# Row turning by transposes, logits and table products in column tiles, one-hots on ScalarE

## Chip, cores and metric

The kernel runs on one core of a Trainium2 chip. The metric is the device time of one execution in microseconds (us), as a median of several runs; less is better.

## What is computed

Two blocks follow each other. The first is a state-space scan (Mamba-2 form) over x (4 batches, 8 heads, 768 tokens, 32 values a head), with a decay per token, and with B and C of 16 state values. The second is a router with eight experts over the 4 x 768 = 3072 rows that come out, each of 8 x 32 = 256 values:

```python
# block 1, per batch and head, over 24 chunks of 32 tokens
L = exp(cum_i - cum_j) * causal
y = (C B^T * L) x  +  (C state) * exp(cum)
state = decay_full * state + sum_j decay_from_j * B_j x_j
# block 2, per row of y
xn = x / (norm(x) + 1e-6);  en = emb / (norm(emb) + 1e-6)
logits = xn @ en.T / tau
e = argmax(logits);  gate = softmax(logits)[e]
out = gate * (relu(x @ w1[e]) @ w2[e])
```

All data are 32-bit floats; w1 is 256 x 1024 and w2 1024 x 256 for each expert.

## The kernel before

**Chunks.** The scan works in six chunks of 128 tokens, each with all four batches at once (`mamba`, L705, loop at L745). One pass of the loop is called a step. In step c TensorE multiplies inside the chunk (`inner`), VectorE masks the products (`mask_inner`, L372), TensorE adds the part from the states (`from_states`) and the outputs (`outputs`, `first_outputs`), and ScalarE copies the result out of PSUM as `yT` (`keep_outputs`, L424), with the 256 values of a row along the partitions. GpSimd scales x and the states (L276, L289, L324); VectorE adds the states up (`add_sums`, L347).

**Rows.** `finish` (L427) turns chunk c − 1 back, so that tokens lie along the partitions. For each batch b and each half z of the 256 values it multiplies `yT` by `turn`, which holds an identity with permuted columns and, beside it, eight columns of the normalised expert embedding: rows and logits come out of one product of 136 columns, in the banks `py[0]`, `py[1]`, `pz[0]`, `pz[1]`. `keep_rows` (L441, L443) copies them to SBUF on ScalarE and `send_rows` writes them to DRAM (`y_rows`). In steps 3 and 4 `finish` is called in two parts, with `locate` between them; in the other steps, and in `scan_end`, in one go.

**Places.** `pick` finds each row's expert (VectorE), `count_picks` counts (GpSimd), `rank_rows` and `keep_ranks` give each row its rank in its expert (TensorE, ScalarE), and `places` (L581, VectorE) turns the rank into a place: a tile of 104 rows (one of four, `NT`) and a place in it (`p`). It makes two one-hots: `eq`, 32 columns (expert, tile) with the row's number, and `hot`, 104 columns with a one at the row's place (L614). `locate` (L620) multiplies them, summed over the four batches of a chunk, to a table of 104 x 32: for each place of each expert the number of the row that goes there. Chunk c − 2 is placed in step c and located one step later. Tables of the first chunks are kept and added (`keep_located` on ScalarE, `add_located` on GpSimd). In the last step `early_places` (L913) makes a first table from three chunks, and GpSimd gathers the first rows of two experts with it. `end_places` (L643) completes the table.

**The scan's end** (`scan_end`, L853) mixes the last chunks' rows and places with the first expert's products, in this order of calls: `up(0)`; ranks of chunk 4; `up(1)`; `finish`, `keep_rows` and `send_rows` of chunk 5; places of chunk 4; pick of chunk 5; `up(2)`, square, `up(3)`, square; `locate` of chunks 3 and 4; `up(4)`; ranks and places of chunk 5; `up(5)`, square, `up(6)`, square; the gates' power, largest and scale; `up(7)`; the second expert's `turn_x`; the gates' exp; `down(0)`; `locate` of chunk 5; `end_places`; the late gathers; `down(1)`. An `up` is four TensorE instructions into one of four PSUM banks, which a Relu on ScalarE (L1049) empties; `down` sums eight such results.

**Experts.** Then `moe` (L1315) takes one expert after the other. Each weight w1 comes as two transfers of 512 KB on the SP queue (`load_weights`, L82), w2 as one of 1 MB; three buffers of each are in use.

**What sets the order.** The scan, `scan_end` and `moe` are under a manual schedule: on every engine, instructions stand in the order in which the code calls them, and an engine takes them in that order. The framework adds the waits for data and for buffers.

Of the kernel before, what the change touches and what calls it, by code (L numbers as in the profile page):

```python
# [16 lines left out]
NB, NH, S, D, N = 4, 8, 768, 32, 16  # L17
# [5 lines left out]
DM, E, F = NH * D, 8, 1024  # L23
KD, KF = DM // 128, F // 128
TR, NT = 104, 4
# [6 lines left out]
LG, Y1, W = 128, 128 + E, DM + E  # L32
# [46 lines left out]
    )  # L79


def load_weights(k, e, parts=(0, 1), after=None):  # L82
    nc = k.nc
    i = slice(e, e + 1)
    if e >= FIXED:
        i = bass.ds(
            nc.values_load(
                k.order[0:1, e - FIXED : e - FIXED + 1], engines=(mybir.EngineType.SP,), min_val=0, max_val=E - 1
            ), 1,
        )  # L90
    if 0 in parts:
        k.w1t[e] = k.wp.tile([128, KD, F], F32, name="w1", tag="w1")
        for v in range(2):
            d = nc.sync.dma_start(
                k.w1t[e][64 * v : 64 * v + 64],
                k.w1[i, 128 * v : 128 * v + 128, :].rearrange("o (z p) f -> p (o z) f", z=KD),
            )
            if after is not None:
                hold(k, d, after)
    if 1 in parts:  # L100
        k.w2t[e] = k.wp.tile([128, KF, DM], F32, name="w2", tag="w2")
        d = nc.sync.dma_start(k.w2t[e][:], k.w2[i].rearrange("o (f p) m -> p (o f) m", p=128))
        if after is not None and 0 not in parts:
            hold(k, d, after)
# [319 lines left out]
        t.kept = k.nc.scalar.copy(out=t.yT[:, z].rearrange("p b s -> p (b s)"), in_=k.py[:, z, :])  # L424


def finish(k, c, parts=(0, 1)):  # L427
    yT = k.ld[c].yT
    banks = (((2, k.py[:, 0]), (3, k.py[:, 1])), ((0, k.pz[0]), (1, k.pz[1])))
    for b, ps in [x for p in parts for x in banks[p]]:  # L430
        for z, at in ((0, 0), (1, LG)):
            k.nc.tensor.matmul(
                ps[:, at : at + Y1], lhsT=yT[:, z, b, :], rhs=k.turn[:, z, :],
                start=(z == 0), stop=(z == 1), skip_group_check=True,
            )


# [23 lines left out]
def square_emb(k):  # L461
    nc = k.nc
    sq = k.mc.tile([E, DM], F32, name="emb_sq")
    r = k.en_r = k.mc.tile([E, 1], F32, name="emb_r")
    nc.scalar.activation(sq[:], k.en[:], ACT.Square, accum_out=r[:])
    nc.gpsimd.tensor_tensor(out=r[:], in0=r[:], in1=k.half[0:E, 0:1], op=ALU.pow)
    k.turn = k.mc.tile([128, KD, Y1], F32, name="turn")
    for z, at in ((0, 0), (1, E)):
        nc.gpsimd.tensor_copy(
            out=k.turn[:, z, at : at + 128].rearrange("p (v r d) -> p v r d", v=2, r=2),  # L470
            in_=k.ident[:].rearrange("p (r v d) -> p v r d", r=2, v=2),
        )


def scale_emb(k):
# [14 lines left out]
def turn_emb(k, ps):  # L490


    nc = k.nc
    for z in range(KD):
        nc.tensor.transpose(ps[:, E * z : E * z + E], k.en2[:, z, :], k.ident[:E, :E])
    for z, at in ((0, 128), (1, 0)):
        nc.scalar.copy(out=k.turn[:, z, at : at + E], in_=ps[:, E * z : E * z + E])


def route_consts(k):  # L500
    nc = k.nc

    def ints(name, shape, pattern, base, by, dtype=F32):
        i = k.mc.tile(shape, I32, name=name + "_i")
        nc.gpsimd.iota(i[:], pattern=pattern, base=base, channel_multiplier=by)
        f = k.const.tile(shape, dtype, name=name)
        nc.gpsimd.tensor_copy(out=f[:], in_=i[:])
        return f

# [12 lines left out]
    k.ones = k.const.tile([128, 128], BF16, name="ones_b")  # L522
    nc.gpsimd.tensor_copy(out=k.ones[:], in_=ones)
    k.before = k.const.tile([128, 128], BF16, name="before_b")
    nc.gpsimd.tensor_copy(out=k.before[:], in_=before)
    k.ob = k.const.tile([128, NU, E], BF16, name="ob")
    k.pre = k.const.tile([128, NU + 1, E], BF16, name="pre")
    nc.gpsimd.memset(k.pre[:, 0, :], 0.0)
    k.s1 = k.const.tile([128, NU], F32, name="s1")
    k.idx = k.const.tile([TR, E * NT], F32, name="idx")  # L530
    k.shifted = k.mc.tile([128, E], F32, name="shifted")
    nc.gpsimd.memset(k.shifted[:], 0.0)
    nc.gpsimd.memset(k.shifted[0:1, 0:2], 1.0)
    k.at, k.eq, k.hot = {}, {}, {}
# [46 lines left out]
def places(k, c):  # L581


    nc = k.nc
    w = k.work
    be = [128, NB, E]
    u = slice(NB * c, NB * c + NB)
    v = k.at.pop(c)
    nc.vector.scalar_tensor_tensor(
        out=v[:], in0=v[:], scalar=1.0, in1=k.ob[:, u, :], op0=ALU.add, op1=ALU.mult  # L590
# [9 lines left out]
    nc.vector.scalar_tensor_tensor(  # L600
        out=p[:], in0=p[:], scalar=-float(TR), in1=k.s1[:, u], op0=ALU.mult, op1=ALU.add
    )
    nc.vector.tensor_tensor(out=v[:], in0=v[:], in1=p[:].unsqueeze(2).to_broadcast(be), op=ALU.subtract)
    eq = k.eq[c] = w.tile([128, NB * E, NT], F32, name="eq", tag="eq")
    nc.vector.tensor_tensor(
        out=eq[:], in0=v[:].rearrange("p b e -> p (b e)").unsqueeze(2).to_broadcast([128, NB * E, NT]),
# [7 lines left out]
    nc.vector.tensor_tensor(  # L614
        out=hot[:], in0=k.place_at[:].unsqueeze(1).to_broadcast([128, NB, TR]),
        in1=p[:].unsqueeze(2).to_broadcast([128, NB, TR]), op=ALU.is_equal,
    )


def locate(k, c, first=True, last=True):  # L620

    eq, hot = k.eq.pop(c), k.hot.pop(c)
    for b in range(NB):
        k.nc.tensor.matmul(  # L624
            k.pz[0][:TR, 424 : 424 + E * NT], lhsT=hot[:, b, :],
            rhs=eq[:].rearrange("p (b e) t -> p b (e t)", b=NB)[:, b], start=(first and b == 0),
            stop=(last and b == NB - 1), skip_group_check=True,
        )


def keep_located(k, c):
    i = k.idx
    if c > 0:
        i = k.ix = k.work.tile([TR, E * NT], F32, name="ix", tag="ix")
    k.nc.scalar.copy(out=i[:], in_=k.pz[0][:TR, 424 : 424 + E * NT])


def add_located(k, c):
    if c > 0:
        k.nc.gpsimd.tensor_tensor(out=k.idx[:], in0=k.idx[:], in1=k.ix[:], op=ALU.add)  # L640


def end_places(k):  # L643
    nc = k.nc
    n = k.pz[1][:, 456 : 456 + E]
    nc.tensor.matmul(n, lhsT=k.ones[:], rhs=k.pre[:, NU, :], start=True, stop=True)
    nc.vector.tensor_tensor(out=k.idx[:], in0=k.idx[:], in1=k.pz[0][:TR, 424 : 424 + E * NT], op=ALU.add)
    k.gi = k.const.tile([TR, E * NT], I32, name="gi")
    k.to = k.const.tile([TR, E * NT], I32, name="to")
    to_rows(k, k.idx[:, 0 : FIXED * NT], 0)  # L650
    k.n = k.const.tile([128, E], F32, name="n")
    nc.vector.tensor_copy(out=k.n[:], in_=n)
# [260 lines left out]
def early_places(k, c):  # L913

    nc = k.nc
    ps = k.pz[0][:TR, 424 : 424 + E * NT]
    locate(k, c)
    nc.vector.tensor_tensor(out=k.idx[:], in0=k.idx[:], in1=ps, op=ALU.add)
    gi = k.ep.tile([TR, E * NT], I32, name="gi0")
    nc.vector.tensor_scalar(out=gi[:], in0=k.idx[:], scalar1=-1.0, scalar2=0.0, op0=ALU.add, op1=ALU.max)  # L920
    k.gi0 = gi


# [562 lines left out]
def leftover(k):  # L1486


    nc = k.nc
# [4 lines left out]
    with k.tc.If(blocks > 0):  # L1494
# [22 lines left out]
        with k.tc.For_i(0, blocks, 1) as i:  # L1517
            e = nc.values_load(table[0:1, 0, bass.ds(i, 1)], engines=(SP,), min_val=0, max_val=E - 1)
            w1 = k.wp.tile([128, KD, F], F32, name="w1", tag="w1")
            for v in range(2):  # L1520
                nc.sync.dma_start(
                    w1[64 * v : 64 * v + 64], k.w1[bass.ds(e, 1), 128 * v : 128 * v + 128, :].rearrange(
                        "o (z p) f -> p (o z) f", z=KD
                    )
                )
# [136 lines left out]
```

## Time and profile before

| | |
|---|---|
| median of three runs | 259.28 us (258.48 to 259.39) |
| the profiled execution | 257.48 us |
| its span, first to last instruction | 255.6 us |
| TensorE (PE) busy | 240.7 us |
| VectorE (DVE) busy | 174.7 us |
| ScalarE (ACT) busy | 109.8 us |
| GpSimd (POOL) busy | 128.4 us |
| turning products, L432 | 96 instructions, 14.0 us |
| table products, L624 | 48 instructions, 5.1 us |

The profile shows one execution. PE counts matmuls, PEld the loading of their weights, which overlaps them. A line such as "L624 PE MATMUL pz<-eq,hot 128*104 128x32 f32 x48 | 5.1, 253" names the line of the code, the engine, what is written from what, the shape, how often, the busy time in us and the mean duration of one in ns; instructions overlap, so the mean is more than the spacing. A 32-bit product appears as two instructions. "idle before" with an arrow tells how long the engine stood still and what released it. The chain of waits is followed back from the last instruction: start, length, what; "issue" is time for which nothing that the profile shows was awaited. In the row of digits each digit is a fortieth of the span, in tenths of busy time.

### The profile page before, as it was taken

How to read it: one execution, taken by the hardware profiler on the slowest of the kernel's cores; microseconds unless marked ns; L12 is line 12 of the kernel's file. 1: busy time of each engine (PE TensorE's matmuls, PEld its weight loads, DVE VectorE, ACT ScalarE, POOL GpSimd, SP SyncE). 2: the span in 40 equal slices, each digit the busy share in tenths (PEclk: the TensorE clock that was granted, in tenths of full speed). 3: DMA queues.
4: the chain of work that ended last, by engine and by line, in shares of the span. 5: the costliest groups of instructions: out<-in, count | busy, mean ns of one | idle time of the engine just before them, and what ended most of it. 6: DMA issues, size and time to landing. Idle time of an engine off the chain costs nothing.

```text
span 255.6 us, 6715 instructions
## 1 busy us (share of the span) xinstructions
PE 240.7 (94%) x2589; PEld 222.5 (87%) x2590; DVE 174.7 (68%) x467; ACT 109.8 (43%) x308; POOL 128.4 (50%) x173
## 2 busy tenths in 40 slices
PE   7889889998999999999999999999999999999990
PEld 2577778878899999999989999999998999999890
DVE  6776898899655533152978897897987888884121
ACT  2435335353254232341385175367338527538300
POOL 8899564764712552838171168248417526026032
PEclk9999999999999999999999999999999999999999
DMA  4978847327299469698911682393194202001001
GB/s 119 306 227 264 279 111 213 131 84 170 65 293 266 151 140 270 147 258 202 255 49 36 135 244 72 88 253 107 39 250 142 69 0 54 11 0 52 13 18 40
DMA packets 22322, 35.90 MB, mean 140 GB/s; under 512 B 2553, under 2 KB 15556, under 8 KB 22288
## 3 DMA queue, kind: packets, MB, share of 16 engines
q1 hardware_dynamic: 19024, 28.73, 41.1%
q0 software_dynamic: 3088, 6.67, 9.8%
q8 instruction: 21, 0.34, 0.6%
q14 instruction: 13, 0.11, 0.1%
q10 hardware_dynamic: 176, 0.06, 0.1%
HBM read 29.05 MB, written 6.50 MB: 139 GB/s over the span
## 4 chain that ended last, share of the span: by engine, by line
PE 46%; POOL 19%; issue 17%; DVE 11%; DMA 5%; ACT 1%; POOLq 1%; DVEq 0%; ACTq 0%
PE yp L1204 15%; PE yp L1132 8%; PE hp L1132 5%; PE eb L1045 5%; DMA out_dram<-yo,to 5%; PE eb L1063 4%; POOL xb L289 4%; POOL xg L934 3%; DVE g L372 3%; POOL out_dram L1255 2%; POOL xs L276 2%; POOL spread L121 1%; PE yp L1032 1%; PE pz L624 1%; PE hp L1045 1%
## 5 line engine op out<-in xcount | busy, mean ns | idle before, releaser
L1255 POOL DMA_INDIRECT out_dram<-yo,to x32 | 34.0, 1063 | 65.1 <-ACT yo L1252 37.2
L934 POOL DMA_INDIRECT xg<-y_rows,gi x32 | 37.3, 1166 | 17.1 <-issue 8.8
L372 DVE TENSOR_TENSOR g<-pg,mask 128x1536 f32<-128x1536 f32 x12 | 21.1, 1754 | 5.5 <-PE pg L362 5.5
L1150 ACT ACTIVATE hT<-hT 128x416 f32<-128x416 f32 (+5 forms) x36 | 19.0, 532 | 12.4 <-DVE hT L1154 11.4
L1063 PE MATMUL yp<-hT,w 128*128 128x208 f32 (+1 forms) x128 | 22.1, 329 | 0.5 <-ACT hT L1150 0.5
L1063 PEld LDWEIGHTS yp<-hT,w 128*128 128x128 f32 x128 | 21.1, 190 | 0.8 <-ACT hT L1150 0.8
L1204 PE MATMUL yp<-T,S 128*128 128x208 f32 (+4 forms) x120 | 21.8, 331 | 0.0
L1282 POOL TENSOR_TENSOR gr<-gr,half 104x4 f32<-104x4 f32 x8 | 9.8, 1219 | 22.0 <-ACT sq L1276 21.9
L1154 DVE TENSOR_TENSOR hT<-hp,u 128x416 f32<-128x416 f32 (+5 forms) x24 | 13.3, 564 | 10.6 <-PE hp L1132 6.5
L1204 PEld LDWEIGHTS yp<-T,S 128*128 128x128 f32 x120 | 20.4, 190 | 0.0
L1132 PE MATMUL yp<-T,S 128*128 128x208 f32 (+5 forms) x96 | 18.6, 336 | 0.4 <-DVE S L1089 0.2
L1132 PEld LDWEIGHTS yp<-T,S 128*128 128x128 f32 x96 | 15.4, 190 | 1.6 <-ACT u L1145 1.1
L1204 PE MATMUL yp<-hT,w 128*128 128x208 f32 (+4 forms) x80 | 15.1, 331 | 0.0
L1145 ACT COPY p<-yp 128x416 f32<-128x416 f32 (+5 forms) x12 | 5.7, 479 | 21.4 <-PE yp L1132 21.4
L1204 PEld LDWEIGHTS yp<-hT,w 128*128 128x128 f32 x80 | 13.7, 190 | 0.0
L1276 ACT ACTIVATE sq<-xg 104x256 f32<-104x256 f32 x32 | 13.0, 408 | 0.0
L1045 PE MATMUL eb<-xT,w 128*128 128x208 f32 x64 | 12.8, 345 | 0.0
L424 ACT COPY yT<-py 128x512 f32<-128x512 f32 x12 | 6.4, 589 | 14.6 <-PE py L413 14.6
L1045 PE MATMUL hp<-xT,w 128*128 128x208 f32 x64 | 12.2, 339 | 0.0
L1063 PE MATMUL eb<-hT,w 128*128 128x208 f32 x64 | 12.0, 341 | 0.0
L1145 ACT COPY u<-yp 128x416 f32<-128x416 f32 (+5 forms) x24 | 11.5, 485 | 1.3 <-PE yp L1132 1.1
L1101 DVE TENSOR_TENSOR T<-hT 128x832 f32<-128x832 f32 (+4 forms) x10 | 9.8, 984 | 3.0 <-ACT hT L1150 3.0
(264 smaller groups left out, 581.3 us busy)
## 6 DMA issues: line engine op xcount, KB each, us to landing
w<-in_moe_w_dram SPq DMA_DIRECT2D x16, 512.0 KB, 6.3
w<-in_moe_w_dram SPq DMA_DIRECT2D x8, 1024.0 KB, 8.2
y_rows<-rows SPq DMA_DIRECT2D x6, 528.0 KB, 5.0
x<-in_x_dram SPq DMA_DIRECT2D x6, 512.0 KB, 6.4
ct<-in_CT_dram SPq DMA_DIRECT2D x6, 256.0 KB, 5.7
bi<-in_BT_dram SPq DMA_DIRECT2D x6, 256.0 KB, 2.8
b<-in_B_dram SPq DMA_DIRECT2D x6, 256.0 KB, 5.2
xa<-in_x_dram SPq DMA_DIRECT2D x6, 128.0 KB, 5.0
```

Source lines behind the costliest of these rows:

```text
L289: engine.tensor_tensor(out=k.xb[c % 2][p, :, :, v, :], in0=src.rearrange("p b (q d) -> p b q d", q=4), in1=r[p, :, 4 * v : 4 * v + 4].unsq ...
L372: t.masked = k.nc.vector.tensor_tensor(out=g[:], in0=k.pg[:, :, 0:384].rearrange("p q (u m) -> p q u m", u=2), in1=k.mask[:].unsqueeze(1). ...
L934: k.nc.gpsimd.indirect_dma_start(out=x, out_offset=None, in_=k.y_d[0:rows, :], in_offset=bass.IndirectOffsetOnAxis(ap=at, axis=0), bounds_ ...
L1045: nc.tensor.matmul(t, lhsT=s.w1[:, j, 128 * f : 128 * f + 128], rhs=s.xT[:, j, 0:m], start=(j == 0), stop=(j == KD - 1))
L1063: nc.tensor.matmul(t, lhsT=s.w2[:, f, 128 * j : 128 * j + 128], rhs=s.hT[:, f, r], start=(f == 0), stop=(f == KF - 1))
L1132: nc.tensor.matmul(t[:, m * u : m * u + m], lhsT=w[:, f : f + 128], rhs=x, start=start and u == 0, stop=True, skip_group_check=True,)
L1145: nc.scalar.copy(out=p[:, 0 : 2 * m], in_=t[:, 0 : 2 * m])
L1150: nc.scalar.activation(h, h, ACT.Relu)
L1154: nc.vector.tensor_tensor(out=h, in0=view(t), in1=view(p), op=ALU.add)
L1204: nc.tensor.matmul(t, lhsT=a[:, f], rhs=b[:, f], start=start and f == 0, stop=(f == 3), skip_group_check=True)
L1255: d = nc.gpsimd.indirect_dma_start(out=k.out[:, :], out_offset=bass.IndirectOffsetOnAxis(ap=s.to[:p, i : i + 1], axis=0), in_=y[:p], in_of ...
L1276: s.k.nc.scalar.activation(sq[:], s.x[:, i, :].rearrange("p (j w) -> p j w", j=KD)[:, :, 0:128], ACT.Square, accum_out=s.r[:, i : i + 1],)
```

## The change

Seven things are edited.

- `finish` turns rows by transposes (one per batch and half) with the plain identity. The values of a row therefore stay in yT's order instead of being permuted.
- The logits are products of their own: the embedding (`emb_t`, padded to 32 columns) times `yT`, one column tile of the array per batch, into `py[0]`. ScalarE copies them to SBUF (`lt`), and four small products turn them into the rows' columns 128 to 135. The transposes of batches 2 and 3 and the logits form part 0, the rest part 1.
- `turn` is gone; `emb_t` is cleared on GpSimd, and one copy on ScalarE instead of two fills it.
- w1 is loaded with its rows permuted to match, by four transfers of 256 KB instead of two of 512 KB.
- `places` makes `hot` on ScalarE: four Squares of (place − p), one per batch, and one Relu of 1 − 2·square. The sign of `p` is turned for that.
- `locate` swaps the operands: `eq` is the stationary one, and each batch has a column tile of its own, so that the sum over batches is not made there. The kept tables are 128 x 104 instead of 104 x 32.
- `table` adds the kept tables to the last one (VectorE) and sums over batches and turns with one product against `same`, four 32 x 32 identities made on GpSimd. `early_places` and `end_places` call it.

```diff
+def w1_rows(k, t, i):
+    issued = []
+    for v in range(2):
+        rows = k.w1[i, 128 * v : 128 * v + 128, :].rearrange("o (z r d) f -> r d (o z) f", z=KD, r=2)
+        for r in range(2):
+            p = 64 * r + 32 * v
+            issued.append(k.nc.sync.dma_start(t[p : p + 32], rows[r]))
+    return issued
...
+def turn_rows(k, c, b, ps):
+    for z, at in ((0, 0), (1, Y1)):
+        k.nc.tensor.transpose(ps[:, at : at + 128], k.ld[c].yT[:, z, b, :], k.ident[:])
...
 def finish(k, c, parts=(0, 1)):
-    yT = k.ld[c].yT
-    banks = (((2, k.py[:, 0]), (3, k.py[:, 1])), ((0, k.pz[0]), (1, k.pz[1])))
-    for b, ps in [x for p in parts for x in banks[p]]:
-        for z, at in ((0, 0), (1, LG)):
+    t = k.ld[c]
+    banks = [k.pz[0], k.pz[1], k.py[:, 0], k.py[:, 1]]
+    if 0 in parts:
+        for b in (2, 3):
+            turn_rows(k, c, b, banks[b])
+        l = k.py[:, 0, W : W + 128]
+        for z in range(KD):
+            for b in range(NB):
+                k.nc.tensor.matmul(
+                    l[32 * b : 32 * b + 32], lhsT=k.emb_t[:, z, :], rhs=t.yT[:, z, b, :], start=(z == 0),
+                    stop=(z == 1), tile_position=(0, 32 * b), skip_group_check=True,
+                )
+        t.lt = k.work.tile([128, 128], F32, name="lt", tag="lt")
+        k.nc.scalar.copy(out=t.lt[:], in_=l)
+    if 1 in parts:
+        for b in (0, 1):
+            turn_rows(k, c, b, banks[b])
+        for b in (2, 3, 0, 1):
+            p = slice(32 * b, 32 * b + 32)
             k.nc.tensor.matmul(
-                ps[:, at : at + Y1], lhsT=yT[:, z, b, :], rhs=k.turn[:, z, :],
-                start=(z == 0), stop=(z == 1), skip_group_check=True,
+                banks[b][:, LG : LG + E], lhsT=t.lt[p], rhs=k.ident[p, 32 * b : 32 * b + E], start=True, stop=True,
+                tile_position=(32 * b, 0), skip_group_check=True,
             )
...
     hot = k.hot[c] = w.tile([128, NB, TR], F32, name="hot", tag="hot")
-    nc.vector.tensor_tensor(
-        out=hot[:], in0=k.place_at[:].unsqueeze(1).to_broadcast([128, NB, TR]),
-        in1=p[:].unsqueeze(2).to_broadcast([128, NB, TR]), op=ALU.is_equal,
-    )
+    for b in range(NB):
+        nc.scalar.activation(hot[:, b, :], k.place_at[:], ACT.Square, bias=p[:, b : b + 1])
+    nc.scalar.activation(hot[:], hot[:], ACT.Relu, bias=1.0, scale=-2.0)
...
     for b in range(NB):
         k.nc.tensor.matmul(
-            k.pz[0][:TR, 424 : 424 + E * NT], lhsT=hot[:, b, :],
-            rhs=eq[:].rearrange("p (b e) t -> p b (e t)", b=NB)[:, b], start=(first and b == 0),
-            stop=(last and b == NB - 1), skip_group_check=True,
+            k.pz[0][32 * b : 32 * b + 32, 400 : 400 + TR],
+            lhsT=eq[:].rearrange("p (b e) t -> p b (e t)", b=NB)[:, b], rhs=hot[:, b, :], start=first, stop=last,
+            tile_position=(0, 32 * b), skip_group_check=True,
         )
...
+def table(k):
+
+    k.nc.vector.tensor_tensor(out=k.idx_t[:], in0=k.idx_t[:], in1=k.pz[0][:, 400 : 400 + TR], op=ALU.add)
+    t = k.pz[1][:TR, 464 : 464 + E * NT]
+    k.nc.tensor.matmul(t, lhsT=k.idx_t[:], rhs=k.same[:], start=True, stop=True, skip_group_check=True)
+    return t
...
-    nc.vector.tensor_tensor(out=k.idx[:], in0=k.idx[:], in1=k.pz[0][:TR, 424 : 424 + E * NT], op=ALU.add)
+    nc.vector.tensor_copy(out=k.idx[:], in_=table(k))
...
     locate(k, c)
-    nc.vector.tensor_tensor(out=k.idx[:], in0=k.idx[:], in1=ps, op=ALU.add)
     gi = k.ep.tile([TR, E * NT], I32, name="gi0")
-    nc.vector.tensor_scalar(out=gi[:], in0=k.idx[:], scalar1=-1.0, scalar2=0.0, op0=ALU.add, op1=ALU.max)
+    nc.vector.tensor_scalar(out=gi[:], in0=table(k), scalar1=-1.0, scalar2=0.0, op0=ALU.add, op1=ALU.max)
```

More of the change, by code (lines that the diff above doesn't have):

```diff
@@ L92, in load_weights @@
         k.w1t[e] = k.wp.tile([128, KD, F], F32, name="w1", tag="w1")
[L93 to L96, printed above, removed]
-            )
+        for d in w1_rows(k, k.w1t[e], i):
             if after is not None:
@@ L466, in square_emb @@
     nc.gpsimd.tensor_tensor(out=r[:], in0=r[:], in1=k.half[0:E, 0:1], op=ALU.pow)
[L467 to L472, printed above, removed]
+    k.emb_t = k.mc.tile([128, KD, 32], F32, name="emb_t")
+    nc.gpsimd.memset(k.emb_t[:], 0.0)
 def scale_emb(k):
@@ L495, in turn_emb @@
         nc.tensor.transpose(ps[:, E * z : E * z + E], k.en2[:, z, :], k.ident[:E, :E])
-    for z, at in ((0, 128), (1, 0)):
-        nc.scalar.copy(out=k.turn[:, z, at : at + E], in_=ps[:, E * z : E * z + E])
+    nc.scalar.copy(out=k.emb_t[:, :, 0:E], in_=ps[:, 0 : KD * E].rearrange("p (z e) -> p z e", z=KD))
 def route_consts(k):
@@ L530, in route_consts @@
     k.idx = k.const.tile([TR, E * NT], F32, name="idx")
+    k.idx_t = k.mc.tile([128, TR], F32, name="idx_t")
+    k.same = k.mc.tile([128, E * NT], F32, name="same")
+    nc.gpsimd.tensor_copy(out=k.same[:], in_=k.ident[:, 0:32])
+    for b in range(1, NB):
+        nc.gpsimd.tensor_tensor(
+            out=k.same[:], in0=k.same[:], in1=k.ident[:, 32 * b : 32 * b + 32], op=ALU.add
+        )
     k.shifted = k.mc.tile([128, E], F32, name="shifted")
@@ L600, in places @@
     nc.vector.scalar_tensor_tensor(
-        out=p[:], in0=p[:], scalar=-float(TR), in1=k.s1[:, u], op0=ALU.mult, op1=ALU.add
+        out=p[:], in0=p[:], scalar=float(TR), in1=k.s1[:, u], op0=ALU.mult, op1=ALU.subtract
     )
-    nc.vector.tensor_tensor(out=v[:], in0=v[:], in1=p[:].unsqueeze(2).to_broadcast(be), op=ALU.subtract)
+    nc.vector.tensor_tensor(out=v[:], in0=v[:], in1=p[:].unsqueeze(2).to_broadcast(be), op=ALU.add)
     eq = k.eq[c] = w.tile([128, NB * E, NT], F32, name="eq", tag="eq")
@@ L613, in places @@
     hot = k.hot[c] = w.tile([128, NB, TR], F32, name="hot", tag="hot")
-    nc.vector.tensor_tensor(
-        out=hot[:], in0=k.place_at[:].unsqueeze(1).to_broadcast([128, NB, TR]),
-        in1=p[:].unsqueeze(2).to_broadcast([128, NB, TR]), op=ALU.is_equal,
-    )
+    for b in range(NB):
+        nc.scalar.activation(hot[:, b, :], k.place_at[:], ACT.Square, bias=p[:, b : b + 1])
+    nc.scalar.activation(hot[:], hot[:], ACT.Relu, bias=1.0, scale=-2.0)
 def locate(k, c, first=True, last=True):
@@ L624, in locate @@
         k.nc.tensor.matmul(
-            k.pz[0][:TR, 424 : 424 + E * NT], lhsT=hot[:, b, :],
-            rhs=eq[:].rearrange("p (b e) t -> p b (e t)", b=NB)[:, b], start=(first and b == 0),
-            stop=(last and b == NB - 1), skip_group_check=True,
+            k.pz[0][32 * b : 32 * b + 32, 400 : 400 + TR],
+            lhsT=eq[:].rearrange("p (b e) t -> p b (e t)", b=NB)[:, b], rhs=hot[:, b, :], start=first, stop=last,
+            tile_position=(0, 32 * b), skip_group_check=True,
         )
 def keep_located(k, c):
-    i = k.idx
+    i = k.idx_t
     if c > 0:
-        i = k.ix = k.work.tile([TR, E * NT], F32, name="ix", tag="ix")
-    k.nc.scalar.copy(out=i[:], in_=k.pz[0][:TR, 424 : 424 + E * NT])
+        i = k.ix = k.work.tile([128, TR], F32, name="ix", tag="ix")
+    k.nc.scalar.copy(out=i[:], in_=k.pz[0][:, 400 : 400 + TR])
 def add_located(k, c):
     if c > 0:
-        k.nc.gpsimd.tensor_tensor(out=k.idx[:], in0=k.idx[:], in1=k.ix[:], op=ALU.add)
+        k.nc.gpsimd.tensor_tensor(out=k.idx_t[:], in0=k.idx_t[:], in1=k.ix[:], op=ALU.add)
+def table(k):
[3 more added lines that the diff above has]
+    return t
 def end_places(k):
@@ L915, in early_places @@
     nc = k.nc
-    ps = k.pz[0][:TR, 424 : 424 + E * NT]
     locate(k, c)
-    nc.vector.tensor_tensor(out=k.idx[:], in0=k.idx[:], in1=ps, op=ALU.add)
     gi = k.ep.tile([TR, E * NT], I32, name="gi0")
-    nc.vector.tensor_scalar(out=gi[:], in0=k.idx[:], scalar1=-1.0, scalar2=0.0, op0=ALU.add, op1=ALU.max)
+    nc.vector.tensor_scalar(out=gi[:], in0=table(k), scalar1=-1.0, scalar2=0.0, op0=ALU.add, op1=ALU.max)
     k.gi0 = gi
@@ L1519, in leftover @@
             w1 = k.wp.tile([128, KD, F], F32, name="w1", tag="w1")
[L1520 to L1525, printed above, removed]
+            w1_rows(k, w1, bass.ds(e, 1))
             w2 = k.wp.tile([128, KF, DM], F32, name="w2", tag="w2")
```

## The prediction

> **What bounds the kernel now.** I read the page's busy shares and slices first, then the chain of waits in order of time, then groups by shape, and last the timeline of ScalarE where the scan ends.
>
> ```profile
> span 255.6 us, 6715 instructions
> PE 240.7 (94%) x2589; PEld 222.5 (87%) x2590; DVE 174.7 (68%) x467; ACT 109.8 (43%) x308; POOL 128.4 (50%) x173
> PE   7889889998999999999999999999999999999990
> ACT  2435335353254232341385175367338527538300
> ```
>
> TensorE is the fullest engine. From slice 11 (about 66 us) it is full nearly to the end, and there every microsecond in which it waits or works more is a microsecond of the kernel. ScalarE looks idle; what counts is what stands behind what in its queue. Before 66 us the chain of waits says something else:
>
> ```profile
> 38.35 1.78 issue
> 40.16 0.63 POOL U L324
> 40.82 0.49 DVE V L347 x2
> 41.31 1.66 DVE g L372
> ...
> 59.79 0.51 DVE hot L614
> 60.34 0.93 PE pz L624 x8
> 61.37 0.20 DVE idx L918
> 61.59 0.18 DVE gi L920
> 61.77 1.67 DVE g L372
> ...
> 81.84 0.67 PE pz L624 x8
> 82.52 2.92 PE eb L1063 x16
> ```
>
> One scan step lasts 10.2 us (U at 29.96, 40.16, 50.49). VectorE works 9.5 of 11 us in 42 to 53 us and TensorE 10.3: they are nearly tied. In the last step the chain runs through the one-hots, the table product and the table, so that stretch has no slack. At 81.84 the last table product is on the chain between the two halves of the first expert's down product.
>
> **What the Trainium skill says.** "ScalarE: Activation LUTs", What ACT_TABLE_LOAD costs: an ACTIVATE takes 186 ns plus 0.833 ns per column, a per-partition scale or bias adds 93 ns, and neighbours overlap by 93. The trace agrees: 128x256 with such a scale took 502 ns (L246; the page gives 492) and started 0.41 apart; Relu on 128x416 took 553 (L1150; 533). "TensorE: Matmul & The Clock Gate", Why this matters for your kernels: small outputs on different column tiles run at the same time. The trace agrees: 64 matmuls of 128*32 by 64 columns (L400) took 1.15 us, 18 ns each, against 34 ns for the two-tile ones of L413. "PSUM — Partial Sum Buffer", PSUM bank collisions: accesses are guarded by bank, not by address. L432's second half waited for the ACT copy of L635 from other columns of the same bank. Same page, Engine vs sequencer instructions: ScalarE's queue is strictly first in, first out; the order below is that of the calls.
>
> **The change part by part.**
>
> ```profile
> L432 PE MATMUL pz<-turn,yT 128*128 128x136 f32 x48 | 7.0, 288 | 1.3 <-DVE V L347 0.7 <-ACT idx L635 0.3 <-ACT ix L635 0.3
> L624 PE MATMUL pz<-eq,hot 128*104 128x32 f32 x48 | 5.1, 253 | 0.4 <-DVE hot L614 0.4
> ```
>
> The 96 records of L432 are 48 products, two passes each: 16 instructions a chunk, 1.86 us when close packed (0.93 per eight in the chain), up to 2.3 in the scan. After: eight transposes, one instruction each as in L1249 (two in 0.22), 0.88; eight logit products in column tiles, 16 instructions of 128 columns. No row shows these; twice L400's 18 ns gives 0.5 (bounds 0.4 and, if tiles do not overlap, 1.7). Four products of 32 rows by 8 columns, like L193's loads, 0.3. Work: 1.7, so 0.15 to 0.6 less per chunk, but a round trip is added: an ACT copy of 128x128 (0.29 by the page) stands between logits and last products, and all three row copies now come after these.
>
> locate: eight instructions took 0.93 (0.67 at 81.84). In column tiles of 104 columns, 0.25. In return table() adds a VectorE sum of 128x104 (0.27, from 0.28 for L347's 128x128), a product (0.1, plus 0.25 until it can be read) and a wait for each.
>
> One-hots: VectorE loses L614, 0.58 (1.01 once). ScalarE gains per chunk four Squares of 104 columns with a bias from memory, 0.366 each, 0.273 apart, then Relu over 416 columns, 0.55 to 0.63: 1.7 us in all. I take 1.7; below, full overlap would leave 1.0; above, none gives 2.1.
>
> w1: two more transfers on SP per expert, 0.61 us each (L94), the same 4 KB rows. SP is idle around them: for w1 of expert 1 the four end at 72.4, before the rows' send (73.17). Weights are asked for over 10 us ahead; without that cover it would cost 1.2 each time. GpSimd's prelude: minus 0.52 (turn), plus a clear (0.1) and `same` (0.2 and three adds of 0.25): +0.5. It delays the first xs from 13.6 to 14.1; TensorE's later 0.85 us wait for VectorE (before 15.76) covers that. Cost 0; uncovered, 0.5.
>
> **The sum in the scan.** Step 1: TensorE reaches inner 0.4 earlier, and VectorE's g was waiting for it: −0.3 to −0.4. Step 2: hot gone, −0.5, but the scan's first half of that gain is partly lost: later row copies delay ScalarE's mask work and the rank copy that places waits for (46.08 before, unmoved). So places starts 0.35 earlier, not 0.78. Its hot was the 1.01 one: T comes 1.3 earlier, and g of step 4 1.2. The table then gives it back. Before, hot ended at 60.3 on VectorE. Now chunk 4's yT copies end at 58.7 (1.2 early), and ScalarE, which does them first, ends the one-hots at 60.4. Locate 60.7, readable 60.95, sum 61.25, table 61.55, gi 61.8: g begins at 61.85 instead of 61.77. TensorE stood behind locate and table meanwhile. Scan: about +0.1.
>
> **The sum where the scan ends**, in the old times:
>
> ```profile
> 69.24 1.07 ACT L424 COPY yT<-py 128x512 f32<-128x512 f32 x2 [0.60 <-PE py L413]
> 70.20 0.36 ACT L1049 ACTIVATE hT<-eb 128x208 f32<-128x208 f32 x1
> 70.44 0.20 ACT L578 COPY rk<-pz 128x32 f32<-128x32 f32 x1
> 70.92 0.34 ACT L1049 ACTIVATE hT<-eb 128x208 f32<-128x208 f32 x1 [0.28 <-PE eb L1045]
> 71.84 0.60 ACT L441 COPY rows<-py 128x528 f32<-128x528 f32 x1 [0.58 <-PE py L432]
> 72.34 0.81 ACT L443 COPY rows<-pz 128x264 f32<-128x264 f32 x2
> ```
>
> After yT (70.3) now come chunk 3's one-hots, to 72.0; behind them the first Relu, the rank copy, the second Relu and the copy lt, to 72.95. Last logit products 73.0 to 73.3 (finish ended at 72.57). Rows are kept by 74.65. Chunk 4's one-hots 74.6 to 76.3; TensorE has done two ups and locate of chunk 3 by 74.9 and waits for them until 76.35. Behind them on ScalarE: Relus 2 and 3, two squares, Relu 4, the rank copy at 78.25. VectorE needs 1.05 for places; the last one-hots run from 79.3 to 81.0. Behind those stand Relu 5, 6, 7 and two squares (ends 81.35, 82.1, 82.85, the last square 82.5). TensorE has finished its ups and the second turn at 79.9, and down(0) waits for its bank, released by Relu 5, from then to 81.4; it ends at 83.35, before 81.84. Locate to 83.6. VectorE's queue now holds the gates' scale ahead of the table's sum. It waits for GpSimd's power, which waits for the last square: 82.6 + 1.2 = 83.8, scale to 84.5, sum to 84.8, product, and down(1) starts at 85.1 instead of 82.52. Loss: 2.5 (2.6, less 0.1 of rounding). TensorE's savings in finish and locate are inside it.
>
> Behind it the expert loop is full on TensorE with unchanged work, so nothing takes the loss back. Late gathers keep some 2 us before the turn at 94.16 and move along. Total 0.1 + 2.5 = **+2.6 us**. The profiled execution took 257.48 us (span 255.6, 1.9 around it), so about 260.1 in its terms; the three timed runs have a median of 259.28, 1.8 above, and the same addition gives **261.9 us**.
>
> **Rivals.** (a) *Faster, at about 257.3.* One mechanism: ScalarE issues the one-hots close together, in 0.9 us or less. Then they are there before TensorE asks; the scan keeps its 1.2, step 5 keeps about 0.5 of locate's saving, and the last section gains 2.07 − 0.75 on locate, less about 1.0 for the table: −2.0. For it: half of ScalarE is idle. Against it: L246 was 0.41 apart at 256 columns, as the page says. It decides near 1.0 us per chunk; each 0.1 more costs about 0.3 in the last section. (b) *No change, 259.6*: the order in the queue bites only half, since Relus and squares lie in stretches where TensorE has a free bank, and scan gain and stalls cancel. (c) *Column tiles do not overlap*: logits 1.7 instead of 0.5 in six chunks, +1.2 times five to six, past 265; L400 speaks against it.
>
> **How the numbers follow.** Main case 0.58, with a range of its own from 260.7 to 263.6 (one-hots 1.4 to 2.0, scan −0.6 to +0.6); (a) 0.22, (b) 0.17, (c) 0.03. A difference of 0.5%, 1.3 us, is about what this measurement can tell from none. Faster 0.22, within 0.18, slower 0.60. The 8-in-10 range reaches into (a): 257.4 to 263.9.
>
> **What would show it.** Right: L614's line on ScalarE, five instructions, 1.5 to 1.9 us a chunk; TensorE gaps of over a microsecond before locate of chunk 4 and in down(0), and a third ahead of down(1), 82 to 87 us; g of step 4 about a microsecond earlier, of step 5 not. Each finish 1.6 to 1.9 of work, locate about 0.25. Wrong: one-hots in about 1 us, no gaps in that stretch, or down(1) starting before 83.

## The result, and the profile after

Four executions of the changed kernel have a median of 266.42 us (266.19 to 267.08); four of the kernel before beside them 258.88. The ratio is 1.0295, with a 95% interval from 1.0264 to 1.0325: 3% slower. The forecast was 261.9 in a range that ended at 263.9. The sign was right, the size was not: the loss is nearly three times the predicted 2.6. The profiled execution has a span of 264.3 us, against 255.6. (The ratios below leave out executions that are over 1.5% above the fastest of the same kernel, so a ratio can be smaller than the medians suggest.)

The page of the changed kernel, its heads and three rows of slices:

```profile
span 264.3 us, 6999 instructions
PE 241.9 (92%) x2690; PEld 219.6 (83%) x2690; DVE 173.0 (65%) x462; ACT 119.4 (45%) x343; POOL 128.6 (49%) x176
PE   6988798896798899999999999999999999999991
ACT  3525345754267522414157248429526436637400
PEclk9999979999979999999999999999999999999997
```

TensorE is busy 1.2 us longer, but the span grew by 8.7: TensorE waits more, and does so in the first fourteen slices. And a row that the prediction did not look at has changed: PEclk has a 7 in the sixth and the twelfth slice. There TensorE ran at half its clock for part of the slice. (The last 7 lies at the very end, where TensorE has hardly any work left.) Before, that row has a 9 in every slice.

The chain of waits of the changed kernel, for the stretch in which the prediction had +0.1 (start, length, what):

```profile
30.64 0.63 POOL U L330
...
35.31 1.81 PE py L389 x32
37.29 1.76 PE py L406 x64
...
43.35 0.48 issue
43.82 0.49 PE py L447 x9
...
52.07 0.69 issue
...
61.70 1.09 ACT hot L643 x4
62.82 0.56 ACT hot L644
63.42 0.43 PE pz L651 x8
...
71.15 0.41 issue
71.57 0.32 PE py L406 x4
71.88 0.41 issue
```

Four things are to be seen. U of step 2 stands at 30.64, where before had 29.96: the scan is 0.7 late already there. L389 took 1.81 and L406 1.76, in the one stretch of half clock; the like products later in the same chain, 32 of L406, took 0.65. At 43.35 and 52.07 TensorE waits for nothing that the profile shows, in the middle of a group of products. And the one-hots, now on ScalarE, stand ahead of the table product at 63.42, as forecast.

The landmarks of TensorE tell where the 8.7 came in. The shift against before is 0.4 at `inner` of step 1, 0.7 at step 2's rows, 1.9 at the first outputs of step 2 (after the half clock), 1.9 and 1.8 at the states of steps 3 and 4, 3.5 when step 5's `finish` is done, 5.1 at the second expert's rows (L1065), 6.6 behind the first expert's `up(0)`, 8.8 at `down(1)`, and 8.8 to the end.

The groups by shape of the changed kernel give the prices of the edits:

```profile
L643 ACT ACTIVATE hot<-place_at,pl 128x104 f32<-128x104 f32 x24 | 7.2, 382 | 1.1 <-DVE pl L628 1.1
L447 PE MATMUL py<-yT,emb_t 128*32 128x128 f32 x96 | 4.1, 279 | 0.5 <-issue 0.5
L644 ACT ACTIVATE hot<-hot 128x416 f32<-128x416 f32 x6 | 3.3, 550 | 0.2
L651 PE MATMUL pz<-hot,eq 128*32 128x104 f32 x48 | 2.3, 261 | 2.6 <-ACT hot L644 2.6
L452 ACT COPY lt<-py 128x128 f32<-128x128 f32 x6 | 1.6, 262 | 6.9 <-PE py L447 6.8
```

Per chunk the one-hots are 7.2/6 + 3.3/6 = 1.75 us, where 1.7 was predicted. The logits are 0.68 of TensorE, their tiles do overlap. The table product fell from 5.1/6 = 0.85 to 0.38. L651 waited 2.6 us for the one-hots in all.

ScalarE's timeline where the scan ends (start, length, engine, line; in brackets what it waited for):

```profile
76.18 1.20 ACT L643 ACTIVATE hot<-place_at,pl 128x104 f32<-128x104 f32 x4
77.41 0.55 ACT L644 ACTIVATE hot<-hot 128x416 f32<-128x416 f32 x1
77.87 0.32 ACT L1082 ACTIVATE hT<-eb 128x208 f32<-128x208 f32 x1
...
85.19 1.20 ACT L643 ACTIVATE hot<-place_at,pl 128x104 f32<-128x104 f32 x4 [1.08 <-DVE pl L628]
86.41 0.55 ACT L644 ACTIVATE hot<-hot 128x416 f32<-128x416 f32 x1
86.87 0.33 ACT L1082 ACTIVATE hT<-eb 128x208 f32<-128x208 f32 x1
```

This is the predicted queue, item by item: the Relus of the first expert stand behind the one-hots. TensorE waited 0.99 before `locate` of chunk 4, 0.92 in `down(0)` for the Relu of 86.87, and 0.27 ahead of `down(1)`.

### The profile page after: what moved, and what is told of

It is laid out like the page before. It is cut to its first block, busy times and chain, and to the rows that moved or that the text cites. A ratio compares the mean times of both kernels' runs of the same rounds, so it can differ in the third digit from the quotient of the medians.

```text
span 264.3 us, 6999 instructions
## 1 busy us (share of the span) xinstructions
PE 241.9 (92%) x2690; PEld 219.6 (83%) x2690; DVE 173.0 (65%) x462; ACT 119.4 (45%) x343; POOL 128.6 (49%) x176
## 4 chain that ended last, share of the span: by engine, by line
PE 35%; issue 28%; POOL 21%; DVE 6%; DMA 4%; ACT 4%; POOLq 1%; DVEq 0%; ACTq 0%
POOL xg L967 9%; POOL out_dram L1288 6%; PE eb L1096 4%; DMA out_dram<-yo,to 4%; PE yp L1165 4%; PE yp L1237 4%; PE eb L1078 3%; PE pg L368 3%; DVE g L378 3%; PE hp L1165 2%; PE py L419 2%; PE py L406 2%; POOL xb L295 2%; POOL xs L282 1%; POOL spread L127 1%
## 5 line engine op out<-in xcount | busy, mean ns | idle before, releaser
L967 POOL DMA_INDIRECT xg<-y_rows,gi x32 | 37.3, 1165 | 16.4 <-issue 8.8
L1187 DVE TENSOR_TENSOR hT<-hp,u 128x416 f32<-128x416 f32 (+5 forms) x24 | 13.3, 563 | 10.6 <-PE hp L1165 5.5
L1237 PEld LDWEIGHTS yp<-hT,w 128*128 128x128 f32 x80 | 13.7, 190 | 0.0
L1078 PE MATMUL eb<-xT,w 128*128 128x208 f32 x64 | 13.5, 358 | 0.0
L583 POOL TENSOR_TENSOR pre<-pre,ob 128x8 bf16<-128x8 bf16 x24 | 4.8, 199 | 17.1 <-DVE ob L578 15.6
```

Of the source, the lines that this page charges most:

```text
L967: k.nc.gpsimd.indirect_dma_start(out=x, out_offset=None, in_=k.y_d[0:rows, :], in_offset=bass.IndirectOffsetOnAxis(ap=at, axis=0), bounds_ ...
L1078: nc.tensor.matmul(t, lhsT=s.w1[:, j, 128 * f : 128 * f + 128], rhs=s.xT[:, j, 0:m], start=(j == 0), stop=(j == KD - 1))
L1187: nc.vector.tensor_tensor(out=h, in0=view(t), in1=view(p), op=ALU.add)
L1237: nc.tensor.matmul(t, lhsT=a[:, f], rhs=b[:, f], start=start and f == 0, stop=(f == 3), skip_group_check=True)
```

## The experiments

**Two theories.** The queue: the one-hots in ScalarE's queue make the loss. Its rival: the loss comes from what the prediction left out, TensorE's clock and its supply of instructions, and those from the other edits. In the expectations Q is the queue and C the clock; two more are F, the new finish with its extra round trip over ScalarE and its later row copies, and P, GpSimd's longer prelude. Throughout, the stretch from `up(0)` to `down(1)`, 13.3 us before and 16.1 after, measures the end of the scan.

**Parts taken back, one at a time.** e1 makes the one-hots on VectorE again, with the old sign of p:

```diff
-    for b in range(NB):
-        nc.scalar.activation(hot[:, b, :], k.place_at[:], ACT.Square, bias=p[:, b : b + 1])
-    nc.scalar.activation(hot[:], hot[:], ACT.Relu, bias=1.0, scale=-2.0)
+    nc.vector.tensor_tensor(
+        out=hot[:], in0=k.place_at[:].unsqueeze(1).to_broadcast([128, NB, TR]),
+        in1=p[:].unsqueeze(2).to_broadcast([128, NB, TR]), op=ALU.is_equal,
+    )
```

> The changed kernel, but with the one-hots made on VectorE by one comparison, as before. Theory Q (the one-hots hold up ScalarE's queue, and TensorE waits behind them in the last scan step, at locate of chunk 4 and in down(0)): the 1.6 us gap before the first table product goes, and the 1.0 and 0.9 us gaps where the scan ends; VectorE pays 0.6 per chunk. 266.4 falls by 3.5 to 4.5, to about 262.4. Theory C (the clock: TensorE runs at half clock for 3.4 us after stretches in which it works little): the second slow window (73 to 76 us) goes as well, because the gap at 62 to 64 us is gone: 5 to 6 less, about 261. Theory F (the extra round trip and the late row copies of finish are what costs): at most 1.5 less.

(These and the later edits are shortened; "..." marks what is left out.) e2 has the old `finish` (turn and its set-up, w1 in two transfers), e3 the old `locate` and tables, without `same`:

```diff
-        turn_rows(k, c, b, banks[b])
...
+        for z, at in ((0, 0), (1, LG)):
+            k.nc.tensor.matmul(ps[:, at : at + Y1], lhsT=yT[:, z, b, :], rhs=k.turn[:, z, :], ...)
```

```diff
-            k.pz[0][32 * b : 32 * b + 32, 400 : 400 + TR], lhsT=eq..., rhs=hot[:, b, :], tile_position=(0, 32 * b), ...
+            k.pz[0][:TR, 424 : 424 + E * NT], lhsT=hot[:, b, :], rhs=eq..., start=(first and b == 0), ...
...
-    nc.vector.tensor_copy(out=k.idx[:], in_=table(k))
+    nc.vector.tensor_tensor(out=k.idx[:], in0=k.idx[:], in1=k.pz[0][:TR, 424 : 424 + E * NT], op=ALU.add)
```

e4 makes `same` in step 1 instead of in the prelude:

```diff
+        if c == 1:
+            build_same(k)
         if n < NC:
             decay_states(k, n)
```

> The changed kernel, but with rows and logits made by the old products with the permuted identity, and w1 in two transfers; one-hots and table product stay as changed. Theory Q: the one-hots still stall TensorE, at most 1 us less, about 265.5. Theory F: rows of batches 2 and 3 are copied early again, spread_ends no longer waits 1.0 us for them, the 0.5 us wait for lt goes: 2 to 3 us less, about 263.8. Theory C: without the gaps at 31 to 34 us TensorE stays at full clock in 35 to 39 us, another 1.2 less.

> The changed kernel, but with the table products as before (104 x 32, summed over batches in the product, no table()), and so without the four small instructions for same in GpSimd's prelude. Theory Q: two waits for the table's sum and product go (about 0.8 each), six table products cost 0.3 to 0.6 more each: between 0.5 less and 1 more, about 266.3. Theory P (GpSimd's prelude delays the whole scan by 0.7): 0.7 less on top of that.

> The changed kernel, but same is made on GpSimd in step 1, where GpSimd waits 2.5 us for VectorE, instead of in the prelude. Theory P: 0.7 less, 265.7, and every landmark of steps 1 to 4 is 0.7 earlier. Theory C: if the earlier first state also shortens the gap at 31 to 34 us by enough, the first slow window goes and it is 1.9 less. If the prelude was covered, nothing moves.

Medians: e1 263.79, ratio 1.0152 [1.0069, 1.0234]; e2 263.62, 1.0131 [1.0053, 1.0209]; e3 266.34, 1.0266 [1.0169, 1.0362]; e4 266.17, 1.0177 [1.0062, 1.0293], with single times from 263.53 to 270.75. Taking back either the one-hots or the finish gives back 2.6 to 2.8, taking back the table nothing. For e2 that is what F said (2 to 3 less); e1 fell by less than Q said (3.5 to 4.5), and e3 and e4 do not show the 0.7 of P in their times. In e4 the prelude's 0.7 is back where it was lost (the state sums start at 13.5 instead of 14.4, `inner` of step 1 at 21.7 instead of 22.7), and yet the kernel is no faster: its profile has 13.6 us at half clock, the changed kernel's 6.8. So something larger than the edits moves the time.

**One part alone.** e8 adds only the one-hots on ScalarE to the kernel before (e1's diff with - and + exchanged, on the old lines), e11 only the finish with emb_t and w1 (e2's likewise), e12 only the tables with `same` in the prelude (e3's likewise).

> The kernel before with one edit of the change alone: the one-hots by four Squares and a Relu on ScalarE. If their place in ScalarE's queue is the main loss, the time rises by 2.2 where the scan ends and by 0.5 to 1.6 in step 5 (VectorE loses 0.6 a chunk, which gives part back): 262 to 263. If they are hidden as the half-idle ScalarE suggests, it stays within 0.7 of the kernel before, or falls; then the loss belongs to the other edits.

> The kernel before with the transposes, the logits in column tiles, the smaller loads of w1 and emb_t alone; one-hots and table as before. If the new finish loses by the borders of the instruction blocks, gaps of 1.5 to 2.7 us in all stand at them, and the time rises to 260.5 to 263. If its smaller work (0.2 to 0.6 a chunk) shows, the time falls by 0.5 to 1.5 below the kernel before.

> The kernel before with the table's column tiles, the copies of 128 x 104 and the identities made in GpSimd's prelude alone; the one-hots stay on VectorE. The prelude costs 0.7 before step 2; locate is 0.3 to 0.5 shorter and the table 0.3 to 0.9 longer. Expected 259.5 to 261; if the sum over batches outside of the table product is what costs, above 262.

e8 262.56 (19 executions, 260.98 to 268.45), 1.0080 [1.0048, 1.0111]; e11 264.19 (4, 260.09 to 265.89), 1.0194 [1.0113, 1.0275]; e12 261.44 (20, 259.56 to 263.61), 1.0070 [1.0041, 1.0099]. All 76 executions of before beside the kernels e1 to e12 have a median of 259.64 and a lowest of 258.29. Each edit is slower alone, by 0.7 to 1.9%; e8 came where it was expected, e11 and e12 somewhat above.

e8 shows the queue theory without the rest. The product before in step 5, TensorE's timeline of e8, then of e6 (below), which has the one-hots on VectorE:

```profile
62.39 0.92 PE L623 MATMUL pz<-eq,hot 128*104 128x32 f32 x8 [1.62 <-ACT hot L616]
```

```profile
61.16 0.39 PE L656 MATMUL pz<-hot,eq 128*32 128x104 f32 x8 [0.68 <-DVE hot L646]
```

In the seven kernels with ScalarE's one-hots and no products put in front of that wait (the changed kernel and its repetition e9, e2, e3, e4, e7, e8) this wait is 1.61 to 1.63, with VectorE's at most 0.68. The end of the scan lasts 15.0 to 16.4 in those with ScalarE's (the longest with `up(0)` partly at half clock), 12.9 to 13.6 in before, e1, e6, e10, e11 and e12. So the queue is real, and worth 1.8 there in e8 against before, at full clock in both. But e11 has none of it and is slower too.

**Clock or waits: products that nobody reads.** e5 is the changed kernel with idle products where TensorE waits; e6 is the changed kernel with e1 and e4 together.

```diff
+def keep_busy(k, n):
+    for _ in range(n):
+        k.nc.tensor.matmul(k.py[:, 1, W:512], lhsT=k.warm[:, 0:Q], rhs=k.warm[:, 0 : 512 - W], start=True, stop=True, ...)
...
+        if c == 1: keep_busy(k, 9)      # after step 2's logits
+            keep_busy(k, 3)             # before spread_ends(k, 1, ...)
+        if c == 4: keep_busy(k, 4)      # before step 5's last logit products
+    keep_busy(k, 14)                    # in early_places, before locate
```

> The changed kernel, with products that nobody reads (bf16, 248 columns, about 0.1 us each) put where TensorE waits for another engine: nine after the logits of step 2, three before the spreading of the ends, fourteen before the table product of step 5 and four before its last logit products. They lie inside waits, so they add no more than about 0.2 us. If the short waits are what lets the granted clock fall to half (the two windows at 35 and at 73 us), the clock stays full and the time falls by the 2.6 us that the windows cost, to about 263.8. If the clock follows something else, or the windows cost nothing, the time stays within 0.7 of 266.4.

> The changed kernel with two things taken back: the one-hots are made on VectorE as before, and GpSimd makes the four identities (same) in step 1 instead of in its prelude. If the queue of ScalarE (1.6 in step 5, 2.2 where the scan ends, less what VectorE's 0.6 a chunk costs) and the prelude (0.7) are the loss, together with the clock windows that come and go, the time falls to 262 to 262.5, and to about 260 if the clock stays full; down(1) starts before 87 and inner of step 1 at 21.7 or earlier. If the new finish and the table themselves cost the time, it stays above 264.

e5: 267.32 (265.59 to 267.97), 1.0266 [1.0186, 1.0347]. The expected fall did not come. In the profiled execution the windows at 35 and 73 us, whose waits were filled, ran at full clock; but another stretch, 45.1 to 52.0, went to half. Just before it, at 41.49, TensorE stood 1.53 us for "issue", in the middle of `inner`; the changed kernel has 0.48 a little further on. So the run speaks for waits as what lowers the clock, in one execution, but not by its time.

e6: 262.25 (12 executions, 259.83 to 265.24), 1.0097 [1.0053, 1.0140]. The time is as expected by the queue and the prelude together (`inner` of step 1, expected at 21.7 or earlier, stands at 22.2). Its profiled execution is one with the clock full to the last slice:

```profile
span 258.1 us, 6984 instructions
PEclk9999999999999999999999999999999999999997
```

The end of the scan is 13.1 and `down(1)` starts at 84.8. What is left of the loss there, 2.4 against before's 82.4, is all in the scan. Gaps with no visible cause at 26.25 (1.02), 32.29 (0.33), 42.0 (0.22), 50.92 (0.47) and 17.09 (0.26) add up to 2.3. They are not simply the 2.4, though: when step 5's products from the states begin, e6 is only 1.0 behind before, so part of the gaps was made up; 1.6 more comes in that step's outputs, with a wait of 0.53 for g and an unexplained gap of 0.44.

**What are the "issue" gaps?** The trace lists every record of TensorE and every DMA packet. Among them are 16 KB packets of a kind called "instruction", 22 of them in the changed kernel, one per 256 of TensorE's records (a load of weights, a product and a wait for a semaphore are one record each). A place where one such block ends is called a border here. Counting records from the start of each trace, the changed kernel's two gaps come after 1729 and 2241 records, e6's five after 448, 960, 1216, 1728 and 2240. All of these leave 192 or 193 when divided by 256. e7 tests whether the gaps belong to that count or to the products around them: the changed kernel with the first warm-up's twelve products of 512 columns in pieces of 128, which puts 70 more records ahead in the same work (a trace misses a few records). e10 does the like to the kernel before, with no part of the change in it:

```diff
-    warm_up(k, 12)
+    for i in range(5):
+        matmul(k.pz[1][:], lhsT=k.warm[:, 0:Q], rhs=k.warm[:], ...)
+    for i in range(63):
+        a = 64 * (i % 8)
+        matmul(k.pz[1][0:32, a : a + 64], lhsT=k.warm[:, 0:32], rhs=k.warm[:, a : a + 64], ...)
```

> The changed kernel, with the twelve 512-column products of the first warm-up as 48 of 128 columns: the same work before any data is there, in 36 products more (36 or 72 records). If the stretches in which TensorE waits for nothing that the profile shows (43.4, 52.1, 70 to 72 us) come from the supply of instructions, which is fetched in blocks of 256, they move to an earlier place in the program: the one that fell in the middle of the logits of step 3 falls 36 to 72 instructions earlier. If something in the logits or in inner itself makes them, they stay where they are in the program. The time itself should stay within 1 us of 266.4.

> The kernel before with nothing of the change: only seven of the twelve first warm-up products, which no one reads, are split, so that 56 products (112 records) more stand ahead of the scan in the same time. If TensorE's instructions come in blocks of 256 records and before happens to have their borders in good places, the borders now fall behind dense stretches: gaps of 0.3 to 1.5 at four to seven of them, index 192 of 256 as in all others, and 1.5 to 4 us more, 261.5 to 264. If the number of instructions ahead doesn't matter, the time stays within 0.7 of the kernel before.

e7: 271.45 in its one execution; the gaps are larger, so the expectation that the time would stay was wrong. Their place was not: they come after 447, 703, 959, 1215 and 1727 records, which is now in other products. The one at 1727 is in `inner` of step 3, no longer in the logits.

e10: 264.21 (20 executions, 260.43 to 270.06), 1.0064 [1.0026, 1.0102]: 1.7 us more by the ratio, 4.6 by the medians. TensorE's timeline of e10 (a profiled execution of 266.51) in step 2's first `inner`, then of before at the same products:

```profile
28.48 0.34 PE L370 MATMUL pg<-cp,bt 32*128 32x64 f32 x4
30.96 0.42 PE L370 MATMUL pg<-cp,bt 32*128 32x64 f32 x2 [2.14 <-issue]
```

```profile
28.48 0.35 PE L362 MATMUL pg<-cp,bt 32*128 32x64 f32 x8
28.65 0.46 PE L362 MATMUL pg<-cp,bi 32*128 32x128 f32 x8
```

At 28.48 the two are level to 0.01 us (a stop of 0.45 in e10, after 449 records, had been made up in a later wait). Then e10 stands 2.14 us with nothing awaited, after 1217 records; again 1.27 after 1729 and 0.29 after 2241. Behind the warm-up the two programs are the same; what differs is how many records lie ahead. The packets show what was missing (from the trace; times in us):

| kernel | border after record | gap | its 16 KB packet | packet's end to gap's end |
|---|---|---|---|---|
| changed | 1728 | 43.35 to 43.83 | 41.3 to 42.5 | 1.33 |
| changed | 2240 | 52.07 to 52.76 | 50.4 to 51.3 | 1.42 |
| e5 | 1728 | 41.49 to 43.02 | 40.3 to 41.4 | 1.67 |
| e7 | 1216 | 31.11 to 33.13 | 30.9 to 31.9 | 1.24 |
| e10 | 1216 | 28.82 to 30.96 | 28.5 to 29.4 | 1.53 |
| before | 2752 | 65.46 to 65.78 | 62.9 to 64.3 | 1.50 |

Up to 85 us the 14 profiles have 163 such borders, with one packet for each, in order. All 32 gaps of over 0.25 us at them end 1.24 to 1.67 us after the packet has landed, and 2.2 to 3.0 after it started; at the 131 others, it had landed at least 1.27 before. TensorE was waiting for its own program. The Trainium skill knows these blocks: "Runtime: NRT & Kernel Launch", Instruction fetch mechanics, gives 256 instructions and 16 KiB a block, fetched while the engine runs, and calls the cost of a border "mostly hidden". The traces agree on the blocks and differ on the cost: where a packet starts late, the gap is up to 2.1 us. Such gaps are rare where the 16 DMA engines are mostly idle (1 of 49 borders with a DMA share under 0.3 in the 3 us ahead), come at 31 of 114 borders above that, and are longest where the share is near 1 (1.27 to 2.14 in e10, 2.02 in e7, 1.53 in e5). What starts a fetch, and whether the DMA engines delay it, was not tested.

By profile, the gaps at borders add up to 0 to 0.32 us in the four kernels with the old finish and before's number of warm-up products (before, e2, e8, e12), to 1.1 to 2.6 in the eight with the new finish and that number, and to 4.2 and 4.4 in e10 and e7. From step 3's rows to step 4's there are 517 records in before and 550 in the changed kernel. With 517, about two blocks, the borders lie at nearly the same place of each step, in before a good one; with 550 they move through the step.

The profile of e11, the new finish alone, is of the fastest of its four executions, with the clock full to the last slice; its span is 258.3 against before's 255.6. It has two stops at borders:

```profile
27.29 1.03 PE L419 MATMUL py<-g,xb 128*64 128x64 f32 x27 [1.45 <-issue]
51.91 0.50 PE L368 MATMUL pg<-cp,bi 32*128 32x128 f32 x7 [0.90 <-issue]
```

It also tells what the finish itself costs (theory F). The finish, with `locate` from step 3 on, stands between the two parts of `inner`. Without the gaps in supply (0.17 in step 3, 0.90 in step 4), the way from one part to the other is 0.2 longer than before in step 3, and 0.1 and 0.3 shorter in steps 4 and 5. So the extra round trip costs next to nothing there. At step 5's second `inner` e11 is 1.3 behind before, and 1.1 more comes in that step's outputs, with gaps of 0.54, 0.33 and 0.27 that are at no border.

**And the clock?** e9 repeats the changed kernel.

> The changed kernel once more, for how its time and the granted clock go together. If the half-clock windows carry part of the loss, its executions lie on a line with the granted clock: those near 0.995 at 263 to 264, those near 0.97 at 266 to 268. If the clock has no part in it, they stay at 266 to 267 whatever the clock.

268.27 (265.73 to 268.97), 1.0304 [1.0211, 1.0397]; with the first four, eight executions with a median of 266.76. None had a mean clock above 0.984, so the expected line could not be drawn: they lie between 265.7 and 269.0 at 0.984 to 0.962 without a clean order. Of before's 76 executions, half have 0.991 or more. e8 has the spread: its six fastest executions, at 0.992 to 0.999, take 260.98 to 261.33, the four at 0.982 to 0.985 take 263.3 to 264.2. In the same kernel, 1.4% less clock went with some 2.7 us more; the waits that come with the lower clock are part of these 2.7.

TensorE's record of the clock changes in steps of 3.41 us. The busy time by such windows of the changed kernel (window, its length, busy us and counts of PE, PEld, DVE, ACT, POOL, then granted clock, DMA share, GB/s):

```profile
28.60:32.00 3.40, 2.30 (x51) 1.75 (x48) 2.60 (x11) 0.65 (x3) 1.36 (x2) 1.00 1.05 328
32.00:35.40 3.40, 2.43 (x51) 2.03 (x53) 2.92 (x8) 2.32 (x7) 1.39 (x3) 1.00 0.13 44
35.40:38.80 3.40, 3.40 (x94) 3.03 (x94) 2.92 (x4) 0.81 (x3) 3.09 (x6) 0.50 0.71 223
...
69.50:72.95 3.45, 2.08 (x56) 1.37 (x45) 1.42 (x6) 0.00 (x0) 2.82 (x6) 1.00 0.20 51
72.95:76.40 3.45, 3.45 (x41) 3.25 (x39) 1.65 (x8) 1.77 (x5) 0.15 (x1) 0.51 0.37 90
```

and of e10, around its long gap at 28.82:

```profile
27.60:31.10 3.50, 1.36 (x46) 1.13 (x38) 2.67 (x12) 1.21 (x4) 1.02 (x2) 0.99 1.05 329
31.10:34.50 3.40, 3.40 (x23) 3.18 (x24) 2.45 (x4) 0.23 (x1) 1.52 (x1) 0.50 0.21 65
```

Windows in which TensorE was busy for 1.36 of 3.50, 2.08 of 3.45 or 2.43 of 3.40 are followed by one at half clock; the one with 2.30 of 3.40 is not. Over 14 profiles, from about 13 to 97 us, the full-clock windows with a busy share up to 0.56 were followed by half clock 9 times of 9, those of 0.56 to 0.72 8 times of about 30, those above never in some 280. The changed kernel's two are of the middle kind, so there the busy share alone does not tell which window is followed by half clock. The new transposes are not needed for it: e2, e8, e10 and e12 turn their rows as before and have half-clock windows before 70 us, and e11, which has the transposes, has none in its profile before the last slice. The page "TensorE: Matmul & The Clock Gate", What's actually happening, has the mechanism: the clock follows how busy the array was in a free-running window of 3.41 us. It names an idle window as what lowers it; here no wait was over 2.2 us, and windows with three to six tenths of waiting, in pieces, were enough. The edges of the windows lie elsewhere in each execution (a half-clock window begins at 35.41 in the changed kernel and at 33.96 in e9), so the same waits can fall into one window or into two. That would explain why the times of one kernel spread by 5 us and more; it was not tested. In e10, where only the supply was disturbed, half clock comes as well, 13.7 us of it in the profiled execution.

None of the kernels was faster than before, and no run pointed to one that would be: e6 with the clock full is still behind, and the one stretch in which it gains, the end of the scan, gains 0.2, less than this measurement can tell.

## Why the prediction was wrong, step by step

- **One-hots 1.7 us: right** (1.75). Rival (a), one-hots in 0.9, is out; (b), no change, is out by the result; and (c) is out too: sixteen logit products in four column tiles took 0.57 to 0.66, not 1.7. Finish and `locate` were sized rightly enough (`locate` 0.36 to 0.43 instead of 0.25).
- **The scan's end, +2.5: right in kind, some 0.5 too large.** Measured +2.0 from `up(2)` to `down(1)` of the changed kernel, +1.8 from `up(0)` in e8, with the three gaps where they were named (0.99, 0.92 and 0.27, for over 1, 1.5 and a third).
- **"Step 1: TensorE reaches inner 0.4 earlier": right but for the next point.** Without `same` in front (e11), `inner` stands at 21.7 instead of before's 22.3.
- **"GpSimd's prelude: +0.5 ... Cost 0; uncovered, 0.5": wrong.** The first xs came at 12.36 instead of 11.64 and TensorE's first state sums at 14.4 instead of 13.8. TensorE's 0.85 wait for VectorE behind them did take that up, as argued. What it could not cover was GpSimd's own queue: GpSimd stayed 0.7 late, U came at 20.86 and 30.64 instead of 20.16 and 29.96, and step 2's rows waited 1.1 for V. The chain of before had shown it, with U of L324 at 40.16.
- **"Scan: about +0.1": wrong, the step that failed most.** When step 5's finish is done the shift is 3.5, behind `up(0)` 6.6. In it are: the prelude 0.7; the one-hots' wait of 1.62 in step 5, which was predicted, but as paid for by a T of step 4 that would be 1.3 earlier (g of step 4 in fact began at 53.32, before at 51.63); and in place of that gain two things for which the sum had no term. Gaps in supply: 0.48, 0.69 and 0.26, where before had one of 0.32. Half clock: two windows of 3.4 us, about 1.2 and 1.4 lost, read from the landmarks on both sides (first outputs of step 2 from +0.7 to +1.9; the first expert's `up(0)`, 1.58 us instead of 0.97, and the first outputs ahead of it, 1.98 instead of 1.15).
- **"Behind it the expert loop ... unchanged work": right**, the shift stays 8.8.

So the mechanism that carried the forecast was right, and costs about what it was said to cost. The sum was too small because every duration in it was taken at full clock and with instructions always at hand. Both held for the kernel before, in its profiled execution, but for one stop of 0.32; in the changed kernel neither held ahead of 77 us.

The parts, as the landmarks of one profiled execution give them: 0.7 prelude, 2.6 half clock, 1.1 more at borders, 1.6 in step 5, 2.2 at the end, and about 1.3 in step 5's last outputs (three "issue" gaps at 70.6 to 72.3 and a wait for g). These are 9.5; the products saved in finish and `locate`, some 0.6 a step of which most was eaten, would take it to 8.7. How the 8.7 divides is thus read off and in part argued: each run that takes one edit back also moves the borders and the half-clock windows. The three gaps at 71 us stay open: they are not at a border, and two of about 0.4 are there in e2, e5, e7, e9 and e12 as well, one in e1 and e6.

## What to carry to other kernels

Where TensorE is nearly full, read its clock row and the "issue" pieces of the chain before adding up durations: a wait of one or two microseconds in a dense stretch can cost twice, once as the wait and once through a following 3.4 us window at half clock (1.2 and 1.4 us here). An edit that adds instructions moves the borders at which the next block of 256 is fetched; where they fall was worth more here (1.7 to 4.6 us in e10, for products without any use) than the edit's own arithmetic; the longest stops came while the DMA engines were full. And where an engine stands first in a chain, as GpSimd does here, half a microsecond in front of its first result is carried on (0.7 at the first two U here) unless a wait behind that result covers it.

## What was not expected of the hardware

- TensorE passed no border of 256 records earlier than 1.24 us after its 16 KB packet had landed (163 borders); where the packet came late it stood, in 32 gaps of 0.26 to 2.14 us.
- The granted clock halved after windows with TensorE 37 to 56% busy, nine times of nine, though no single wait was over 2.2 us.
- With products without a reader put into the waits (e5), the clock stayed full in the windows that they filled and fell elsewhere, behind a longer stop at a border; they too move the borders.
